# Two decode layers with a cached attention: where two weight blocks and two kept quarters lie, and how one V load is split

## The chip, the cores and the metric

The kernel runs on one core of a Trainium2 chip. The time is the device time of one execution in microseconds (us); of several runs the median is given. In the traces, TensorE is PE (its weight loads PEld), VectorE is DVE, ScalarE is ACT, and SP is the engine that issues the loads.

## The reference

One token goes twice through the same two blocks: attention with 32 heads over a cache of 4096 keys and values, and a small MLP. All is float32.

```python
# x (1,1,512); k_cache, v_cache (1,32,4096,128); wq (512,4096); wo (4096,512)
def A(x, k, v, wq, wo):
    q = (x @ wq) per head                       # (1,32,1,128)
    p = softmax(q . k * 128**-0.5)
    return (p . v) over all heads @ wo
def B(x, w1, b1, w2, b2):
    return gelu(x @ w1 + b1) @ w2 + b2
x = x + A(layernorm(x), ...)
x = x + B(layernorm(x), ...)
x = x + A(layernorm(x), ...)
x = x + B(layernorm(x), ...)
```

The cache is 134 MB. Both layers read it, and what fits into the core's memory between the two isn't read again.

## The kernel before

**Tiles.** The heads are worked on in 8 groups of 4. K or V of one group is a block of 128 partitions by 16384 elements (8.39 MB). It is cut into 8 chunks, and a chunk into 4 quarters, one for each head of the group. `U` is the width of a quarter (512), `NC = 4 * U` that of a chunk. So a place such as `C_AT + 22 * U` lies in the middle of chunk 5 of block C. wq and wo of one group take a chunk's room each; two such that lie side by side in memory are loaded as one `pair` (2.10 MB).

**Places.** One large tile, `arena`, holds three blocks A, B and C, and behind them `SHARED`, a scratch place and `PAIR`, where the pair lies at most times.

**A group.** `scores` multiplies the queries with K, chunk by chunk (4 matmuls for a chunk). `exponentials` and `weights` make the softmax on VectorE and ScalarE and turn it with 4 transposes on TensorE. `values` multiplies with V, again 8 chunks of 4 matmuls. `head_out` projects with wo (4 matmuls), and `next_queries` makes the next group's queries with wq (4 matmuls). TensorE does this in program order.

**Order of the loads.** `load` issues a DMA on SP's queue, in program order. SP waits with each load until the place it writes is free, that is until the last reader of all that it covers has ended; the loads behind it wait along with it. Loads of the K and V blocks go round A, C and B.

**The second layer** goes through the groups backwards, 7 to 0. K of group 7 is still in C and V of group 7 in A, from the first layer. Of V of group 6, 26 quarters were kept in B and the last 6 in PSUM (`pK`). While the scores of group 7 run over C, K of group 6 is loaded into `SHARED`, behind the pair, and into the chunks of C that become free, up to 22U. The pair of wo and wq for group 6 and 5 comes behind it. Then ScalarE copies the 6 kept quarters out of PSUM, two of them into C and four to `PAIR`, and with them group 6 has all that it needs.

With `n = 2`, group 5 begins: its K goes into A, which is free as soon as the values of group 7 have been taken. Its V goes into C, over K of group 6, the pair and the two kept quarters. It is loaded in two parts, and each part waits for its own readers:

```python
for c, t in blocks(v, g, v_home, LAST if final else ((0, 5), (5, 8)) if n == 2 else ((0, C),)):
```

All other blocks up to the last group are loaded whole.

Of the kernel before, what the change touches and what calls it, by code (L numbers as in the profile page):

```python
# [23 lines left out]
C = 8  # L24
# [4 lines left out]
U = 512  # L29
# [7 lines left out]
A_AT, B_AT, C_AT = RING  # L37
# [3 lines left out]
PAIR = SHARED + 11 * U  # L41
# [3 lines left out]
LAST = ((0, 4), (4, 6), (6, 7), (7, 8))  # L45
# [5 lines left out]
def decode_layers(ctx: ExitStack, tc: tile.TileContext, x, k, v, w, w1, b1, w2, b2, out):  # L51
# [13 lines left out]
    def at(first, n):  # L65
        return arena[:, first : first + n]

    def load(first, src):
        t = at(first, src.shape[-1])
        tc.keep_in_program_order(nc.sync.dma_start(t, src))  # L70
        return t
# [4 lines left out]
    def quarters(first):  # L76
        return [at(first + U * j, U) for j in range(4)]

    def part(src, g, a, b):
        return src[g][:, NC * a : NC * b]  # L80

    def of_w(row, i, n):
        return w[row][:, NC * i : NC * (i + n)]

    def by_four(t):
        return t.rearrange("p (j n) -> p j n", j=4)
# [67 lines left out]
    def idle(to, n=U):  # L154
        matmul(to[:, :n], zero[:, 0:1].to_broadcast([P, P]), at(C_AT, n), start=True, stop=True)
# [34 lines left out]
    def scores(z, c, kt):  # L190
        for j in range(J):
            matmul(pS[32 * j : 32 * j + C, :], z[:, j, C - 1 - c : 2 * C - 1 - c], kt[j],
                   start=(c == 0), stop=(c == C - 1))

    def exponentials(sc, nsc):
        nc.vector.tensor_reduce(ml[:, 0:1], pS, axis=AX.X, op=ALU.max)  # L196
        mt, m, bias = small("mt", 32), small("m"), small("mt", 32)
        nc.vector.transpose(mt, ml)
        nc.vector.tensor_reduce(m, mt[:, :C], axis=AX.X, op=ALU.max)
        nc.vector.tensor_scalar(mb[:, :C], m.to_broadcast([P, C]), nsc, None, op0=ALU.mult)  # L200
        nc.vector.transpose(bias, mb)  # L201
        p = at(SCRATCH, U)
        nc.scalar.activation(p, pS, AF.Exp, bias=bias[:, 0:1], scale=sc, accum_out=ml[:, 0:1])  # L203
        return p

    def weights(p):
        for b in range(4):
            tc.keep_in_program_order(nc.tensor.transpose(  # L208
                pT[:, b].rearrange("p j r -> p (j r)"), p[:, P * b : P * (b + 1)], ident))
        pt = work.tile([P, P], F32, name="turned").rearrange("p (j c b) -> p j c b", j=J, c=C)  # L210
        nc.vector.tensor_copy(pt, pT[:, :, :, :C].rearrange("p b j c -> p j c b"))  # L211
        lt, l, lr, rl = small("mt", 32), small("l"), small("mt", 32), small("rl")
        nc.vector.transpose(lt, ml)  # L213
        nc.vector.tensor_reduce(l, lt[:, :C], axis=AX.X, op=ALU.add)
        nc.vector.tensor_copy(lb, l.to_broadcast([P, 32]))
        nc.vector.transpose(lr, lb)
        nc.vector.reciprocal(rl, lr[:, 0:1])
        return pt, rl

    def values(i, pt, vt, c):  # L220
        for j in range(J):
            matmul(pO[32 * j : 32 * j + 4, :], pt[:, j, c, :], vt[j],
                   start=(i == 0), stop=(i == C - 1))

    def head_out(rl, wt, last=False):
        ot = at(SCRATCH, U)
        nc.vector.transpose(ot, pO)  # L227
        o, on = small("o", 4), on_wide
        own = at(SCRATCH, 4 * 129).rearrange("p (b q) -> p b q", q=129)[:, :, :P]
        own = own.rearrange("p b (d q) -> p d b q", q=32)[:, :, :, 0]  # L230
        nc.vector.tensor_reduce(o, own, axis=AX.X, op=ALU.add)  # L231
        if last:
            nc.vector.tensor_scalar(on[:, :4], o, rl, None, op0=ALU.mult)
        else:
            nc.vector.tensor_scalar(in_quarters(on, 4), o.unsqueeze(1).to_broadcast([P, J, 4]), rl, None,  # L235
                                    op0=ALU.mult)
        for d in range(4):
            if last:
                for j in range(J):
                    matmul(pS[32 * j : 32 * j + 1, :P], on[:, d : d + 1], wt[:, d, P * j : P * (j + 1)],  # L240
                           start=(d == 0), stop=(d == 3))
            else:
                matmul(pO, on[:, d : d + P], wt[:, d, :], start=(d == 0), stop=(d == 3))
        return of_32(turned(pS) if last else turned(pO, wide=True), 4)
# [34 lines left out]
    def load_w1(first, a, b):  # L279
        load(first + W1C * a, w1[:, W1C * a : W1C * b])  # L280

    def load_w2(first, a, b):
        load(first + U * a, w2[:, U * a : U * b])
# [4 lines left out]
    def blocks(src, g, home, pieces=((0, C),)):  # L288
        for a, b in pieces:
            load(home + NC * a, part(src, g, a, b))  # L290
            for c in range(a, b):
                yield c, quarters(home + NC * c)
# [15 lines left out]
    def next_queries(n, xs, negm, wt):  # L308
        for c in range(4):
            matmul(pO, xs[:, 2 * c : 2 * c + P], wt[:, c, :], start=(c == 0), stop=(c == 3))  # L310
        return queries(n, negm, wide=True)

    def add_up(acc, own):
        t = small("acc", 4)
        nc.vector.scalar_tensor_tensor(t, own, 1.0, acc, op0=ALU.mult, op1=ALU.add)
        return t
# [4 lines left out]
    for g in range(G):  # L321
        final = g == G - 1
        k_home, v_home = RING[2 * g % 3], RING[(2 * g + 1) % 3]
# [3 lines left out]
        for c, t in blocks(v, g, v_home, LAST if final else ((0, C),)):  # L327
# [3 lines left out]
            if g == G - 2:  # L331
                for j in range(J):
                    i = 4 * c + j - KEPT_V // U
# [8 lines left out]
        else:  # L342
            pair = load(PAIR, of_w(g % 2, g, 2))
# [11 lines left out]
    g = G - 2  # L355
# [5 lines left out]
    def begin_k(home, n):  # L361
        a = len(k_t)
        load(home, k[g][:, U * a : U * (a + n)])
        k_t.extend(at(home + U * i, U) for i in range(n))
# [4 lines left out]
    for c in range(C):  # L369
# [2 lines left out]
            begin_k(C_AT + NC * c, 4)  # L372
        if c == 5:
            begin_k(C_AT + 2 * NC, 14)
    pair = load(C_AT + 22 * U, of_w(g % 2, g - 1, 2))
    p = exponentials(sc, nsc)
    z = next_queries(1, xs, negm, wq_t)
    pt, rl = weights(p)
# [2 lines left out]
    acc = add_up(acc, head_out(rl, wo_t))  # L381

    v_t = [at(B_AT + U * i, U) for i in range(KEPT_V // U)]
    for i, first in enumerate([C_AT + 30 * U, C_AT + 31 * U] + [PAIR + U * j for j in range(4)]):
        t = at(first, U)
        nc.scalar.copy(t, pK[i])
        v_t.append(t)
# [9 lines left out]
    for n in range(2, G):  # L397
        g, final = G - 1 - n, n == G - 1
        k_home, v_home = homes[(2 * n - 1) % 3], homes[2 * n % 3]
        for c, t in blocks(k, g, k_home, HALVES if final else ((0, C),)):  # L400
            scores(z, c, t)
        pt, rl = weights(exponentials(sc, nsc))
        for c, t in blocks(v, g, v_home, LAST if final else ((0, 5), (5, 8)) if n == 2 else ((0, C),)):
            values(c, pt, t, c)
            if final and c > 4:
                idle(pS)
        if final:
            wo_t = by_four(load(PAIR, of_w(g % 2, g, 1)))
            for a, b in W1_AT_END:
                load_w1(A_AT, a, b)  # L410
            for a, b in W2_AT_END:
                load_w2(A_AT + 11 * U, a, b)
            own = head_out(rl, wo_t, last=True)
        else:
            pair = load(PAIR, of_w(g % 2, g - 1, 2))
            acc = add_up(acc, head_out(rl, by_four(pair[:, NC:])))
            z = next_queries(n + 1, xs, negm, by_four(pair[:, :NC]))
# [47 lines left out]
```

## Time and profile before

| | |
|---|---|
| median of 3 runs | 680.22 us (679.94 to 680.78) |
| the profiled execution | 679.55 us, its span 677.8 us |
| TensorE busy | 433.1 us, 64% |
| VectorE busy | 110.7 us, 16% |
| ScalarE busy | 22.2 us, 3% |
| read from HBM | 286.14 MB |
| mean rate over the span | 422 GB/s |

The span runs from the first to the last instruction of the trace. The shares of the engines are means over it. The rate is what the 16 DMA engines of the core read.

### The profile page before, as it was taken

The numbers are of one execution on the slowest core, as the hardware profiler recorded it, in microseconds if no ns is written. First come the engines' busy times: TensorE is split into PE (matmuls) and PEld (weight loads), VectorE is DVE, ScalarE is ACT, GpSimd is POOL, SyncE is SP. The second block draws the span as 40 slices with busy tenths as digits, with TensorE's granted clock in tenths as the row PEclk, the third lists the DMA queues.
The fourth block names the chain that finished last, engine by engine and source line by source line (L and its number), as shares of the span: only waits on it lengthen the run. The fifth ranks groups of instructions, "written<-read, shape, count | busy, mean of one in ns | idle before, by whom it ended". The sixth has DMA issues, their size and how long they took to land. (4 is left out here: it accounts for less than half of the span.)

```text
span 677.8 us, 6359 instructions
## 1 busy us (share of the span) xinstructions
PE 433.1 (64%) x2792; PEld 119.4 (18%) x2792; DVE 110.7 (16%) x431; ACT 22.2 (3%) x47; POOL 4.3 (1%) x21
## 2 busy tenths in 40 slices
PE   1547666485554874667777897686455764766776
PEld 0112112121111211111113222221111111211112
DVE  1012101111021101210212312211021011210211
ACT  0010000000000000001000110000000000000000
POOL 1000000000000000000000000000000000000000
PEclk9969768797698876977979998998698776977977
DMA  9999999999999999999999999899999999999997
GB/s 372 434 433 433 435 433 433 416 449 437 430 433 413 451 433 430 433 431 422 428 413 359 426 459 414 358 468 441 427 433 398 465 433 423 437 430 410 426 416 294
DMA packets 11404, 286.56 MB, mean 423 GB/s; under 512 B 1776, under 2 KB 1776, under 8 KB 3440
## 3 DMA queue, kind: packets, MB, share of 16 engines
q1 hardware_dynamic: 10944, 286.14, 98.7%
q8 instruction: 22, 0.36, 0.2%
q10 hardware_dynamic: 432, 0.01, 0.0%
q14 instruction: 6, 0.05, 0.0%
HBM read 286.14 MB, written 0.00 MB: 422 GB/s over the span
## 5 line engine op out<-in xcount | busy, mean ns | idle before, releaser
L74 PE MATMUL pO<-arena,turned 128*4 128x512 f32 x1024 | 144.8, 726 | 76.8 <-DMA arena<-in_v 75.6
L74 PE MATMUL pS<-arena,zq 128*8 128x512 f32 x1024 | 137.7, 698 | 70.8 <-DMA arena<-in_k 65.4
L74 PE MATMUL pO<-arena,x_wide 128*128 128x512 f32 (+1 forms) x176 | 54.9, 508 | 24.4 <-DVE turned L137 18.1
L74 PE MATMUL pO<-arena,on_wide 128*128 128x512 f32 x112 | 51.8, 605 | 18.6 <-DVE on_wide L235 18.6
L74 PEld LDWEIGHTS pS<-arena,zq 128*8 128x8 f32 x1024 | 29.1, 99 | 176.3 <-issue 167.1
L74 PEld LDWEIGHTS pO<-arena,turned 128*4 128x4 f32 x1024 | 27.6, 97 | 183.8 <-issue 179.5
L137 DVE STREAM_TRANSPOSE turned<-pO 32x128 f32<-32x128 f32 x112 | 35.0, 312 | 101.1 <-PE pO L74 99.9
L227 DVE STREAM_TRANSPOSE arena<-pO 128x512 f32<-128x512 f32 x16 | 11.5, 717 | 220.4 <-PE pO L74 220.4
L208 PE MATMUL pO<-ident,arena 128*128 128x128 f32 x64 | 14.5, 368 | 43.9 <-ACT arena L203 42.4
L196 DVE TENSOR_REDUCE ml<-pS 128x1 f32<-128x512 f32 x16 | 11.1, 692 | 185.0 <-PE pS L74 185.0
L74 PEld LDWEIGHTS pO<-arena,x_wide 128*128 128x128 f32 (+1 forms) x176 | 21.6, 155 | 57.1 <-DVE turned L137 26.5
L203 ACT ACTIVATE arena<-pS,mt,sc 128x512 f32<-128x512 f32 x16 | 12.4, 777 | 523.7 <-DVE mt L201 523.7
L74 PEld LDWEIGHTS pO<-arena,on_wide 128*128 128x128 f32 x112 | 20.1, 189 | 51.7 <-DVE on_wide L235 31.6
L208 PEld LDWEIGHTS pO<-ident,arena 128*128 128x128 f32 x64 | 9.3, 181 | 58.6 <-ACT arena L203 51.3
L74 PE MATMUL pO<-arena,x 128*2 128x344 f32 x64 | 7.2, 531 | 5.0 <-DMA arena<-in_w 4.4
L74 PE MATMUL pS<-arena,zero 128*128 128x512 f32 x16 | 9.9, 706 | 0.0
L74 PE MATMUL pS<-arena,gelu_g 128*1 128x128 f32 x176 | 6.7, 290 | 1.5 <-DVE gelu_g L270 1.3
L213 DVE STREAM_TRANSPOSE mt<-ml 128x32 f32<-128x32 f32 x16 | 3.4, 212 | 17.2 <-ACT arena L203 17.2
L74 PEld LDWEIGHTS pS<-arena,gelu_g 128*1 128x1 f32 x176 | 3.9, 88 | 7.4 <-DVE gelu_g L270 3.7
L211 DVE COPY turned<-pO 128x128 f32<-128x128 f32 x16 | 4.4, 277 | 3.1 <-PE pO L208 3.1
L74 PE MATMUL pO<-arena,zero 128*128 128x512 f32 x8 | 4.5, 644 | 0.0
L248 POOL TENSOR_TENSOR xb<-x,b2c 128x4 f32<-128x4 f32 x2 | 0.4, 200 | 636.9 <-DVE x L148 636.9
(71 smaller groups left out, 76.5 us busy)
## 6 DMA issues: line engine op xcount, KB each, us to landing
arena<-in_w SPq DMA_DIRECT2D x13, 2048.0 KB, 28.8
arena<-in_k SPq DMA_DIRECT2D x4, 4096.0 KB, 42.5
arena<-in_v SPq DMA_DIRECT2D x2, 4096.0 KB, 47.6
arena<-in_w SPq DMA_DIRECT2D x6, 1024.0 KB, 20.3
arena<-in_v SPq DMA_DIRECT2D x1, 5120.0 KB, 23.8
arena<-in_w SPq DMA_DIRECT2D x6, 688.0 KB, 30.2
arena<-in_v SPq DMA_DIRECT2D x2, 2048.0 KB, 50.8
arena<-in_v SPq DMA_DIRECT2D x4, 1024.0 KB, 53.3
```

The lines of the kernel that those rows point to most:

```text
L74: tc.keep_in_program_order(nc.tensor.matmul(*a, **kw))
L137: nc.vector.transpose(t[q], src[q, P * j : P * (j + 1)])
L196: nc.vector.tensor_reduce(ml[:, 0:1], pS, axis=AX.X, op=ALU.max)
L203: nc.scalar.activation(p, pS, AF.Exp, bias=bias[:, 0:1], scale=sc, accum_out=ml[:, 0:1])
L208: tc.keep_in_program_order(nc.tensor.transpose(pT[:, b].rearrange("p j r -> p (j r)"), p[:, P * b : P * (b + 1)], ident))
L211: nc.vector.tensor_copy(pt, pT[:, :, :, :C].rearrange("p b j c -> p j c b"))
L213: nc.vector.transpose(lt, ml)
L227: nc.vector.transpose(ot, pO)
L248: nc.gpsimd.tensor_tensor(xb, pairs(xs)[:, :, 0], b2c, op=ALU.add)
```

## The change

The pair of wo and wq for group 6 and 5 moves from 22U to 24U of C: from the half of chunk 5 to chunks 6 and 7. The first two of the kept quarters of V of group 6 move from 30U and 31U (the end of chunk 7) to 22U and 23U (the second half of chunk 5). V of group 5 is loaded as chunks 0 to 5 and 6 to 7, where it was 0 to 4 and 5 to 7. Nothing else changes; what is computed, and from which bytes, is the same.

```diff
-    pair = load(C_AT + 22 * U, of_w(g % 2, g - 1, 2))
+    pair = load(C_AT + 24 * U, of_w(g % 2, g - 1, 2))
...
-    for i, first in enumerate([C_AT + 30 * U, C_AT + 31 * U] + [PAIR + U * j for j in range(4)]):
+    for i, first in enumerate([C_AT + 22 * U, C_AT + 23 * U] + [PAIR + U * j for j in range(4)]):
...
-        for c, t in blocks(v, g, v_home, LAST if final else ((0, 5), (5, 8)) if n == 2 else ((0, C),)):
+        for c, t in blocks(v, g, v_home, LAST if final else ((0, 6), (6, 8)) if n == 2 else ((0, C),)):
```

On SP, the difference of the two programs from the pair for group 6 (first row) to K of group 4 (last row) is this; a name that begins with DMAHW is the landing of an earlier load, the other names are the counts of an engine's finished work:

```order
 L70 DMA arena<-in_w 128x4096 [waits PE_49]
 L70 DMA arena<-in_k 128x16384 [waits DMAHW0_49,PE_49]
-L70 DMA arena<-in_v 128x10240 [waits DMAHW5_49,DMAHW4_49,DMAHW6_49,DMAHW1_49,PE_49]
-L70 DMA arena<-in_v 128x6144 [waits DMAHW2_49,DMAHW7_49,PE_49,Activation_49]
+L70 DMA arena<-in_v 128x12288 [waits DMAHW4_49,DMAHW5_49,DMAHW1_49,DMAHW6_49,PE_49,Activation_49]
+L70 DMA arena<-in_v 128x4096 [waits DMAHW7_49,DMAHW2_49,PE_49]
 L70 DMA arena<-in_w 128x4096 [waits DMAHW3_49,Activation_49]
 L70 DMA arena<-in_k 128x16384
```

The order of the loads stays. The wait for ScalarE, whose copies fill the kept quarters, has moved from the second part of V to the first; the first part now covers their place, and so it waits for the values that read them. The row of the pair is the same.

On TensorE, in the values of group 5, the difference is this:

```order
 L208 MATMUL pO<-ident,arena 128x128 x3
 L74 MATMUL pO<-arena,turned 4x512 [waits DMAHW1_49,DVE_49]
-L74 MATMUL pO<-arena,turned 4x512 x19
+L74 MATMUL pO<-arena,turned 4x512 x23
 L74 MATMUL pO<-arena,turned 4x512 [waits DMAHW2_49]
-L74 MATMUL pO<-arena,turned 4x512 x11
+L74 MATMUL pO<-arena,turned 4x512 x7
 L74 MATMUL pO<-arena,on_wide 128x512 [waits DMAHW3_49,DVE_49]
 L74 MATMUL pO<-arena,on_wide 128x512 x3
```

The matmuls are the same. The wait for the second part of V has moved from the first matmul of chunk 5 to the first of chunk 6.

## Rows read from the trace of the kernel before

**Rows 1.** The page: TensorE's busy time; DMA share in 40 slices, in tenths.

```profile
PE 433.1 (64%) x2792; PEld 119.4 (18%) x2792; DVE 110.7 (16%) x431; ACT 22.2 (3%) x47; POOL 4.3 (1%) x21
DMA  9999999999999999999999999899999999999997
```

**Rows 2.** Windows: length, engines' busy us (instructions); last PE clock, DMA share, GB/s.

```profile
4.00:345.00 341.00, 201.29 (x1164) 54.39 (x1168) 50.39 (x191) 11.41 (x23) 0.99 (x4) 0.82 1.00 431
426.00:436.00 10.00, 8.36 (x63) 2.42 (x65) 1.48 (x5) 0.00 (x0) 0.00 (x0) 1.00 0.82 319
416.00:446.00 30.00, 22.53 (x144) 6.44 (x136) 6.65 (x24) 0.87 (x2) 0.00 (x0) 0.94 0.97 406
445.00:645.00 200.00, 126.03 (x716) 33.67 (x708) 31.90 (x114) 4.16 (x10) 0.00 (x0) 0.83 1.00 432
```

**Rows 3.** TensorE's waits from 445 us on: us in total, times, longest.

```profile
PE pO L74 <- DMA arena<-in_v: 28.7, 5, 7.4
PE pS L74 <- DMA arena<-in_k: 18.9, 5, 5.0
```

**Rows 4.** The chain that ended last, its end: start, us, what.

```profile
655.95 17.85 DMA arena<-in_w
...
675.29 0.17 DVE y L421
```

**Rows 5.** Timeline of SP: start and length of an issue, us.

```profile
394.39 0.33 SPq L70 DMA_DIRECT2D arena<-in_k  x1
...
406.36 0.33 SPq L70 DMA_DIRECT2D arena<-in_v  x1
...
428.80 0.33 SPq L70 DMA_DIRECT2D arena<-in_v  x1
...
429.65 0.43 SPq L70 DMA_DIRECT2D arena<-in_k  x1
```

**Rows 6.** Issue to landing, us: issues at 394.39, 406.36, 428.80; first load; output.

```profile
arena<-in_k SPq DMA_DIRECT2D x1, 23.7
...
arena<-in_v SPq DMA_DIRECT2D x1, 5120.0 KB, 23.8
...
arena<-in_v SPq DMA_DIRECT2D x1, 3072.0 KB, 9.8
...
arena<-in_w SPq DMA_DIRECT2D x1, 1024.0 KB, 5.1
...
out<-y SPq DMA_DIRECT2D x1, 2.0 KB, 1.4
```

**Rows 7.** Timeline of TensorE: values of groups 7, 6; scores, values 5; scores 4.

```profile
387.27 7.05 PE L74 MATMUL pO<-arena,turned 128*4 128x512 f32 x64 [0.39 <-DVE turned L211]
...
410.19 8.40 PE L74 MATMUL pO<-arena,turned 128*4 128x512 f32 x64 [0.38 <-DVE turned L211]
...
430.35 7.05 PE L74 MATMUL pS<-arena,zq 128*8 128x512 f32 x64 [1.64 <-DVE zq L186]
...
441.55 8.09 PE L74 MATMUL pO<-arena,turned 128*4 128x512 f32 x64 [0.38 <-DVE turned L211]
...
464.49 8.56 PE L74 MATMUL pS<-arena,zq 128*8 128x512 f32 x64 [4.74 <-DMA arena<-in_k]
```

**Rows 8.** Timeline of ScalarE: two kept quarters copied, and the exponential behind.

```profile
381.28 1.07 ACT L386 COPY arena<-pK 128x512 f32<-128x512 f32 x2 [16.46 <-PE pS L74]
382.96 0.78 ACT L203 ACTIVATE arena<-pS,mt,sc 128x512 f32<-128x512 f32 x1 [0.60 <-DVE mt L201]
```

**Rows 9.** Timeline of the weight loads: last of group 6's scores and values.

```profile
405.29 0.11 PEld L74 LDWEIGHTS pS<-arena,zq 128*8 128x8 f32 x4 [0.32 <-issue]
...
416.70 0.10 PEld L74 LDWEIGHTS pO<-arena,turned 128*4 128x4 f32 x4 [0.33 <-issue]
417.13 0.10 PEld L74 LDWEIGHTS pO<-arena,turned 128*4 128x4 f32 x4 [0.33 <-issue]
417.56 0.10 PEld L74 LDWEIGHTS pO<-arena,turned 128*4 128x4 f32 x4 [0.33 <-issue]
```

## The prediction

> **What bounds the kernel now.** Read the page first. TensorE is busy 64% of the span, while the DMA line stands at 9 in all slices but two [rows 1]. The reader is to see a kernel that is one long stream of loads. Next come the windows: the stream moves 431 GB/s from 4 to 345 us and 432 from 445 to 645, with a DMA share of 1.00 [rows 2]. From 445 us on TensorE waits five times for a K load and five times for a V load, so every one of the five groups left waits for its loads [rows 3]; and the chain that ended last closes with a 17.85 us wait for the last weights and under 2 us of work behind it [rows 4]. So a microsecond in which the stream stands still in the second layer is a microsecond at the end, and nothing else counts.
>
> The change touches one place where it does stand still. In 426 to 436 us the rate is 319 GB/s; over 416 to 446 it is 406 [rows 2]. Against 432 that is 10 x (1 - 319/432) = 2.6 us and 30 x (1 - 406/432) = 1.8 us of standstill. The issues of the loads say why [rows 5, 6]. K of group 5 (8.39 MB) is issued at 394.39 and lands 23.7 us later, at 418.1. The first part of V of group 5 (5.24 MB) is issued at 406.36 and lands at 430.2: 12.1 us behind K, which is just 5.24 MB at 432 GB/s, so the stream runs on without a hole. The second part (3.15 MB) is issued only at 428.80 and lands at 438.6: 8.4 us behind the first, where its bytes need 7.3. Its place holds wo and wq, and the last projection that reads them ends just before 428.8, as the scores of group 5 begin at 430.35 behind a transpose [rows 7]. By the landings, which the slowest engine sets, the hole is 1.1 us; by bytes over all engines 1.8 to 2.6. From issue to landing the second part took 9.8 us, that is 2.5 us beyond its bytes: this I call the restart.
>
> **The change, part by part.**
>
> The pair of wo and wq moves from 22U to 24U in C. Before and after it overlaps chunk 7 of the scores, so its issue waits for the same matmuls (in the listing its row is the same). Cost 0.
>
> Two kept quarters go to 22U and 23U, in chunk 5. Their copies may start two chunks of scores (7.05 us for eight chunks [rows 7]) or 1.8 us sooner than at 381.28. ScalarE has nothing else until the exponential at 382.96 [rows 8], and values of group 6, which read the copies, begin at 410.19 [rows 7]. Cost and gain 0; were that cover gone, two copies cost 1.07 us.
>
> The split of V of group 5 at six chunks makes the first part 6.29 MB and the second 2.10 MB, the same bytes. The two are still issued one behind the other on SP, and behind them stand the next pair and K of group 4 (429.65) [rows 5]. What changes is which reader frees each. The second part still covers the pair, so it is still free at 428.80. The first part now covers 22U and 23U. These hold the kept quarters 26 and 27, and they are read by chunk 6 of the values of group 6. So the first part no longer goes out behind the scores, at 406.36, but behind chunk 6 of the values.
>
> When is that? The weight loads of these values stand in groups of four, two for a chunk; the last chunk's are at 417.13 and 417.56, chunk 6 ends with the one at 416.70 [rows 9]. From the last group to the issue that it frees takes 1.07 us, as the scores show (405.29 to 406.36) [rows 5, 9]. So the first part is issued at 416.70 + 1.07 = 417.8, 11.4 us later than now.
>
> At that time only 0.3 us of K of group 5 are left (it lands at 418.1), and SP has issued nothing behind it. The old cover, 11.7 us of K still to come at 406.36, is gone, and the stream stops here instead. With the restart of 2.5 us the first part lands at 417.8 + 2.5 + 6.29 MB/432 GB/s = 417.8 + 2.5 + 14.6 = 434.9. A stream without a hole would have landed it at 418.1 + 14.6 = 432.7, so the new hole is 2.2 us. In return the old one closes: at 428.80 the first part has 6 us to go, the second part follows without a gap, 4.9 us for 2.10 MB, and lands at 439.7. Now it lands at 438.6. All that follows is 1.1 us later.
>
> The same sum, shorter: both kernels restart the stream once, at 428.80 or at 417.8. After the later restart 3.15 MB of V remain, after the earlier one 8.39. The difference of 5.24 MB takes 12.1 us, and TensorE needs only 428.80 - 417.77 = 11.0 us between the two releases. 12.1 - 11.0 = **+1.1 us**. The restart cancels if it costs the same at both places.
>
> TensorE itself loses nothing: values of group 5 start at 441.55 and take 8.09 us [rows 7], so they need the first part by 441.55 (lands 434.9) and the second, now at chunk 6 and not 5, by about 447 (lands 439.7).
>
> **Bounds.** The trace has no restart from a queue that is all but empty in this place. The nearest rows: the 2 KB output took 1.4 us from issue to landing, and the first load of the program, 1.05 MB, 5.1 us, that is 2.7 beyond its bytes [rows 6]. With 1.4 the sum is 0.0, with 2.7 it is +1.3. I take 2.5, since it is the same queue, the same kind of transfer and the same engines 11 us away. The moment of release hangs on TensorE's clock: these values took 8.40 us, those of group 7 took 7.05 at 387.27 [rows 7]. Were they 1.35 us quicker in another execution, the first part would go out at 416.4, but the projection behind them would end 1.35 us sooner too, for either kernel: the difference of 1.1 stays, and the time would come to -0.25 against the before seen here.
>
> The rate is the other term. The rows give 431 and 432 GB/s over 341 and 200 us [rows 2]. The Trainium skill, "DMA: Bandwidth & Descriptors", section "Where 436 GB/s comes from", says that for transfers from HBM to SBUF the HBM side, about 358 GB/s, binds, and not the fabric's 435. By that figure K of group 5 would still be under way long after 417.8, neither split would leave a hole, and the sum would be 0. The trace does not agree: 432 is near the page's fabric figure, and the hole is there.
>
> **The numbers.** The profiled execution took 679.55 us, 677.8 of it the span and 1.75 around it; it should become 680.6. It lies 0.67 below the median of the runs, 680.22, so the median should become 680.22 + 1.1 = **681.3 us**. I count as no change what is within 0.2%, 1.36 us; +1.1 is 0.16%.
>
> **Rivals.**
>
> Faster: the hole closes and none opens. Place: the issue of the first part. To follow K of group 5 without a gap it would have to go out by 415.6 (418.1 less the restart). Then the second part lands 1.1 us sooner by the landings, 1.8 to 2.6 by bytes: 677.6 to 679.1, about 678.4. For it: the bigger first part does cover the wait at 428.80. Against it: the release at 417.8 is 2.2 us too late, and even the quicker values give 416.4. Chance 0.07.
>
> Slower by over 0.2%: a restart out of an empty queue costs more than the one seen, where 1.4 us of the first part were still in flight at 428.80. From 2.8 us up the loss passes 1.36 us. With the first load's 2.7 it is 681.5, with 3.2 it is 682.0. For it: the first load is the only one that starts on an empty queue. Against it: 2.7 and 2.5 lie close. Chance 0.21.
>
> No difference: K of group 5 lands late enough to cover the new wait, or the restart is as cheap as the output's 1.4 us. It would need K to land 2.2 us later than its row, at 420.3, or a slower stream; then before would have no hole either. 680.2. Chance 0.05. (The rule of the Trainium skill's DMA page above ends here; the rows on the rate speak against it.)
>
> **How the numbers follow.** The forecast, +1.1 us and within 0.2%, has 0.67. Same: 0.67 + 0.05 = 0.72; slower 0.21; faster 0.07. The range goes from the cheap restart (680.2) less the 0.3 by which the fastest run lies under the median, 679.9, to the dear one (681.5) plus the 0.6 by which the slowest lies above it, 682.1. It holds all but the faster rival and the ends of the slower one, under 2 in 10.
>
> **What the profile after will show.** The first part of V of group 5 (6144 KB) issued near 417.8, released by matmuls into pO, 17 us to landing; the second (2048 KB) near 428.8, about 11 us to landing. The rate falls in 414 to 422 and is full in 426 to 436. Scores of group 4, which now wait for their K until 464.49 [rows 7], start about 1.1 us later, and so does each stage behind; the two copies of ScalarE start near 379.5. An issue of the first part at 416 or sooner, or scores of group 4 no later than now, would make the prediction wrong; so would a shift at the end that is not there at group 4.

## The result, and the profile after

The changed kernel takes 681.73 us in the median, the kernel before 680.43 in the same comparison (22 runs each): a ratio of 1.0018, with a 95% interval from 1.001 to 1.0027. By the ratio that is 1.2 us slower, from 0.7 to 1.8. The forecast was +1.1.

The profiled execution of the changed kernel has a span of 680.1 us. These are its lines on TensorE's share and on the DMA engines in 40 slices, from the page:

```profile
PE 429.3 (63%) x2792; PEld 119.3 (18%) x2792; DVE 110.4 (16%) x431; ACT 22.2 (3%) x47; POOL 4.3 (1%) x21
DMA  9999999999999999999999998999999999999996
```

One slice is at 8 again, but it is another one: the 25th (408 to 425 us) and no longer the 26th (424 to 441) [rows 1]. The windows show the same move (columns as in [rows 2]); the first row is of the kernel before, the four others of the changed one:

```profile
414.00:422.00 8.00, 6.67 (x49) 1.93 (x42) 1.13 (x3) 0.00 (x0) 0.00 (x0) 1.00 0.92 396
414.00:422.00 8.00, 6.67 (x50) 1.91 (x39) 1.13 (x3) 0.00 (x0) 0.00 (x0) 1.00 0.78 299
426.00:436.00 10.00, 8.36 (x62) 2.31 (x64) 1.48 (x5) 0.00 (x0) 0.00 (x0) 1.00 0.96 410
416.00:446.00 30.00, 22.53 (x132) 6.50 (x128) 6.65 (x24) 0.87 (x2) 0.00 (x0) 0.89 0.95 399
445.00:645.00 200.00, 126.33 (x720) 33.91 (x712) 31.39 (x112) 3.48 (x8) 0.00 (x0) 0.83 1.00 431
```

From 426 to 436 us the stream now runs at 410 GB/s, where it ran at 319; from 414 to 422 it stands still for a part of the time (299, where it was 396). From 445 us on it is full as it was. The 30 us around both show 399 GB/s in place of 406, but that difference decides nothing: a kernel below that loads as before does (the places alone) has 392 and 390 there.

The timeline of SP shows the issues of K of group 5 and of the two parts of its V, and below it is the time from issue to landing of each, in the same order:

```profile
394.18 0.33 SPq L70 DMA_DIRECT2D arena<-in_k  x1
...
417.61 0.33 SPq L70 DMA_DIRECT2D arena<-in_v  x1
...
428.49 0.33 SPq L70 DMA_DIRECT2D arena<-in_v  x1
```

```profile
arena<-in_k SPq DMA_DIRECT2D x1, 25.9
...
arena<-in_v SPq DMA_DIRECT2D x1, 6144.0 KB, 18.5
...
arena<-in_v SPq DMA_DIRECT2D x1, 2048.0 KB, 12.5
```

The first part went out 11.3 us later than in [rows 5], the second 0.3 sooner. On TensorE and ScalarE these rows of the timeline belong to it (the end of chunk 6, the values of group 5, the scores of group 4; the two copies):

```profile
416.46 0.10 PEld L74 LDWEIGHTS pO<-arena,turned 128*4 128x4 f32 x4 [0.33 <-issue]
...
441.38 9.55 PE L74 MATMUL pO<-arena,turned 128*4 128x512 f32 x64 [0.38 <-DVE turned L211]
...
465.35 9.52 PE L74 MATMUL pS<-arena,zq 128*8 128x512 f32 x64 [4.29 <-DMA arena<-in_k]
```

```profile
379.35 1.07 ACT L386 COPY arena<-pK 128x512 f32<-128x512 f32 x2 [14.75 <-PE pS L74]
```

The last group of weight loads of chunk 6 is at 416.46; 1.07 us later is 417.53, and the issue came at 417.61. The values of group 5 waited for the softmax and not for a load. The copies started 1.9 us sooner, and nothing followed from that.

The executions differ by a microsecond or two before they come to this place, so one number serves for all kernels below: **the stage**, from the issue of K of group 5 (TensorE sets it, at the end of group 7's values) to the first scores of group 4, which wait for their K. Before it is 464.49 - 394.39 = 70.1 us [rows 5, 7]; in the changed kernel it is 465.35 - 394.18 = 71.2. The difference is +1.1 us.

A second number goes with it. The trace holds 16 marks for the landing of each load, the updates of the load's semaphore, which no view prints one by one. They are read here as one for each of the 16 DMA engines. The time from issue to landing in the views, and with it the stage, goes by the last mark alone. For K of group 4 the marks lie between 462.19 and 464.35 us before and between 463.26 and 465.21 in the changed kernel. **The mean mark** of K of group 4, counted from the issue of K of group 5 as the stage is, tells where the whole stream stands and not its slowest engine: 68.3 us before, 69.8 in the changed kernel, a difference of +1.4.

### The profile page after: what moved, and what is told of

It reads as the page before. It is cut to its first block, busy times and chain, and to the rows that moved or that the text cites. A ratio compares the mean times of both kernels' runs of the same rounds, so it can differ in the third digit from the quotient of the medians.

```text
span 680.1 us, 6360 instructions
## 1 busy us (share of the span) xinstructions
PE 429.3 (63%) x2792; PEld 119.3 (18%) x2792; DVE 110.4 (16%) x431; ACT 22.2 (3%) x47; POOL 4.3 (1%) x21
## 5 line engine op out<-in xcount | busy, mean ns | idle before, releaser
L74 PE MATMUL pO<-arena,turned 128*4 128x512 f32 x1024 | 143.1, 719 | 80.7 <-DMA arena<-in_v 79.5
## 6 DMA issues: line engine op xcount, KB each, us to landing
arena<-in_v SPq DMA_DIRECT2D x1, 6144.0 KB, 18.5
```

The lines of the kernel that those rows point to most:

```text
L74: tc.keep_in_program_order(nc.tensor.matmul(*a, **kw))
```

## The experiments

The theory on trial: the second layer is a stream of loads, and what counts is when it restarts after it has run dry, and how many bytes are left then. The rivals: the new places cost by themselves (theory 2), or the sizes of the two parts do (theory 3). All kernels were timed against the kernel before, with the stage and the mean mark read from one profiled execution of each.

| kernel | first part out, us | second (third) | stage, us | mean mark, us | against before: ratio (interval) | us |
|---|---|---|---|---|---|---|
| before | 406.4 | 428.8 | 70.1 | 68.3 | 1 | |
| changed | 417.6 | 428.5 | 71.2 | 69.8 | 1.0018 (1.001 to 1.0027) | +1.2 |
| changed, again | 417.9 | 428.8 | 71.4 | 69.7 | 1.0018 (1.0004 to 1.0032) | +1.2 |
| places alone | 407.8 | 430.6 | 69.9 | 68.7 | 0.9987 (0.9974 to 1.0001) | -0.9 |
| places alone, again | 407.5 | 430.2 | 70.0 | 68.6 | 1.0 (0.9986 to 1.0013) | 0.0 |
| split alone | 427.1 | 428.8 | 80.1 | 78.6 | 1.0134 (1.012 to 1.0148) | +9.1 |
| chunk 6 last | 419.0 | 429.0 | 72.1 | 70.6 | 1.0031 (1.0018 to 1.0044) | +2.1 |
| chunk 6 first | 412.8 | 429.6 | 69.5 | 67.0 | 0.998 (0.9967 to 0.9992) | -1.4 |
| three parts | 407.8 | 419.9 (430.4) | 67.6 | 66.7 | 0.9986 (0.9972 to 0.9999) | -1.0 |
| three parts, again | 406.5 | 418.4 (428.9) | 68.3 | 66.8 | 0.9983 (0.9971 to 0.9995) | -1.2 |
| cut at 22U | 406.9 | 429.6 | 71.1 | 67.7 | 0.9997 (0.9987 to 1.0007) | -0.2 |
| cut at 22U, again | 406.4 | 430.3 | 70.3 | 68.6 | 0.9989 (0.9976 to 1.0002) | -0.7 |

The last column is the ratio by the 681 us of before. The stage and the mean mark don't always agree, since the last mark of K of group 4 came 0.8 to 3.3 us behind the mean one. Where they differ the mean mark is the better guide: from it to the mean mark of the last weights it took 210.7 us in all twelve executions, within 0.04 us, so what the stream has lost or gained by K of group 4 stands unchanged at its last load.

**One half of the change at a time.** The places alone, with the old split:

```diff
-        ... LAST if final else ((0, 6), (6, 8)) if n == 2 else ((0, C),)):
+        ... LAST if final else ((0, 5), (5, 8)) if n == 2 else ((0, C),)):
```

> The pair and the two kept quarters lie as in the changed kernel, but V of group 5 is split at chunk 5 as before. Theory 1, the loss is the time in which the load stream stands still because the first part waits for chunk 6 of the values: the first part is free behind the scores again (issue near 406.4), the second near 428.8, the hole is the old one, and the time is that of before, 0.0 us. Theory 2, the new places cost by themselves (copies, waits on ScalarE, other addresses): slower than before by 1.2 us, as the whole change was.

The stage came to 69.9 us, that of before. The whole was 0.9 us faster, with an interval that just took in 1; so it was run again:

> The new places with the old split a second time: 0.9 us faster than before the first time, with an interval that just takes in no change. If the places do nothing: 69.9 us from the issue of K of group 5 to the scores of group 4 as the first time, and an interval around 0.0 us. If they gain by themselves (copies that may start sooner): again 0.9 us faster.

Stage 70.0, ratio 1.0. No cost and no gain of the places is seen. The second interval reaches 0.9 us either way, and the +1.2 of theory 2 lies outside both, so theory 2 falls. The first part was free behind the scores in both; its issue in the first:

```profile
407.81 0.33 SPq L70 DMA_DIRECT2D arena<-in_v  x1
```

The split alone, with the places of before:

```diff
-        ... LAST if final else ((0, 5), (5, 8)) if n == 2 else ((0, C),)):
+        ... LAST if final else ((0, 6), (6, 8)) if n == 2 else ((0, C),)):
```

> The places of before, and only the split at chunk 6. The first part now covers half of wq, so it is freed by the second matmul of the last projection, near 427.9. Theory 1: the stream restarts at 427.9 with 8.39 MB of V to go instead of at 428.8 with 3.15 MB: 12.1 - 0.9 = 11.2 us slower than before. Theory 3, the sizes of the two parts cost by themselves: slower by about 1.2 us only, as the whole change was.

It cost 9.1 us (8.2 to 10.1), the stage 10.0. The windows and the timeline of SP of this kernel show a stream that stands still for 10 us and more:

```profile
416.00:426.00 10.00, 7.28 (x39) 2.32 (x28) 2.54 (x8) 0.00 (x0) 0.00 (x0) 1.00 0.00 0
```

```profile
427.05 2.11 SPq L70 DMA_DIRECT2D arena<-in_v  x2
```

The size is that of theory 1 and not the 1.2 of theory 3, but the expectation was 1.2 too high, and the timeline says why: the first part was out at 427.05, not at 427.9. The part covers the first two chunks of wq, and the second of the projection's four steps of 0.93 us (3.70 us in all) frees it, not the third. Counted from the issue of K of group 5, that is 32.5 us, and the second part of before went out at 34.4. With that, 12.1 - (34.4 - 32.5) = 10.2 us; the stage shows 10.0 and the mean mark 10.3.

**When the first part is freed.** Two kernels are the changed one, with its places and its sizes, but with the values of group 6 in another order of chunks. Chunk 6 first:

```diff
-    for c in range(C):
-        values(c, pt, v_t[4 * c : 4 * c + 4], c)
+    for i, c in enumerate((6, 0, 1, 2, 3, 4, 5, 7)):
+        values(i, pt, v_t[4 * c : 4 * c + 4], c)
```

> The changed kernel, its places and its split at chunk 6, but the values of group 6 take chunk 6 first, then 0 to 5 and 7 (the sum is over the same products in another order). The kept quarters at 22U and 23U are read first, so the first part is freed near 411.9 and not 417.7. Theory 1: K of group 5 covers the restart and no hole is left in either place: faster than before by 1.1 to 2.6 us, and than the changed kernel by 2.3 to 3.8. Theories 2 and 3: as the changed kernel, +1.2 us.

Chunk 6 last, where the order is (0, 1, 2, 3, 4, 5, 7, 6):

> The changed kernel, but the values of group 6 take chunk 6 last (0 to 5, 7, 6), so the kept quarters are read 0.9 us later and the first part is freed near 418.5 in place of 417.6. Theory 1: the stream restarts 0.9 us later with the same 8.39 MB to go. From the issue of K of group 5 to the first scores of group 4 (70.1 us before, 71.2 in the changed kernel) it takes 72.0 us, and the whole is 1.9 to 2.1 us slower than before. Theory 3 (sizes of the parts): as the changed kernel, 71.2 us and +1.2.

The kernel with chunk 6 last was 2.1 us slower than before (1.2 to 3.0), its stage 72.1 us where 72.0 was expected. Its first part went out here:

```profile
418.96 0.33 SPq L70 DMA_DIRECT2D arena<-in_v  x1
```

The one with chunk 6 first was 1.4 us faster than before (0.5 to 2.2), with the same bytes in the same two parts at the same places; so theory 3 falls too. Its stage is shorter by only 0.6, its mean mark by 1.3: the last mark was 2.4 us behind the mean one in this execution, where it was 1.6 before. Here are the issue of its first part and its window:

```profile
412.77 0.33 SPq L70 DMA_DIRECT2D arena<-in_v  x1
```

```profile
416.00:446.00 30.00, 22.52 (x144) 6.29 (x136) 6.57 (x24) 0.87 (x2) 0.00 (x0) 0.94 0.99 418
```

The stream moves 418 GB/s over the 30 us, against 399 and 386 in the changed kernel and 381 with chunk 6 last. From first to last the order of eight chunks is worth 3.5 us.

**Three parts.** Then the new places do have a use: the first part as before, chunk 5 by itself, and chunks 6 and 7.

```diff
-        ... LAST if final else ((0, 6), (6, 8)) if n == 2 else ((0, C),)):
+        ... LAST if final else ((0, 5), (5, 6), (6, 8)) if n == 2 else ((0, C),)):
```

> The new places, and V of group 5 in three parts: chunks 0 to 4, chunk 5, chunks 6 and 7. Theory 1: the first part is issued near 406.4 (behind the scores), the second near 417.7 (behind chunk 6 of the values), while the first is still under way to 430, the third at 428.8 with 3.7 us of the stream still to go. No hole but perhaps a small one, as a restart took 2.5 us: faster than before by 1.1 us (by the landings) to 2.6 (by the bytes). Theories 2 and 3 (places or sizes cost): not faster than before, +1.2 us.

> The kernel in three parts a second time, since its first interval reached from 0.9972 to 0.9999. Theory 1: 67.6 us from the issue of K of group 5 to the scores of group 4, as the first time, within 1 us, and 1.1 to 2.6 us faster than before over the whole. If the gain of the stage is given back later: the same 67.6 us, and no difference over the whole.

The window, the issues of V of group 5 and the scores of group 4 in the first of the two:

```profile
416.00:446.00 30.00, 22.53 (x141) 6.28 (x136) 6.58 (x24) 0.87 (x2) 0.00 (x0) 0.94 1.02 427
```

```profile
407.79 12.47 SPq L70 DMA_DIRECT2D arena<-in_v  x2
...
430.44 0.33 SPq L70 DMA_DIRECT2D arena<-in_v  x1
```

```profile
463.42 7.05 PE L74 MATMUL pS<-arena,zq 128*8 128x512 f32 x64 [1.96 <-DMA arena<-in_k]
```

No hole is left (427 GB/s; 433 in the second). The stage was 2.5 us shorter than before, 1.8 the second time. The whole was 1.0 and 1.2 us faster, at the lower end of what was expected (the first just under it), with both intervals below 1. This kernel and the one with chunk 6 first beat the kernel before, and by the ratios the changed one too. Of the gain of the stage 0.6 to 1.5 us did not reach the end: behind the stage this kernel took 678.0 - 463.42 = 214.6 us in the profile, before took 677.8 - 464.49 = 213.3. The stream gave nothing back. The mean mark had gained only 1.7 and 1.5 us, which lies in both intervals of the whole, and it kept that gain to the last weights. The rest of the stage's 2.5 was the last engine, 0.8 us behind the mean here and 1.6 before.

**Fewer bytes behind the same restart.** The places of before, and V cut where K of group 6 ends, so that the second part has 2.62 MB and not 3.15:

```diff
+    def in_two(src, g, home, n):
+        load(home, src[g][:, :n])
+        load(home + n, src[g][:, n:BLOCK])
+        for c in range(C):
+            yield c, quarters(home + NC * c)
...
-        for c, t in blocks(v, g, v_home, LAST if final else ((0, 5), (5, 8)) if n == 2 else ((0, C),)):
+        vt = blocks(v, g, v_home, LAST if final else ((0, C),))
+        for c, t in in_two(v, g, v_home, 22 * U) if n == 2 else vt:
             values(c, pt, t, c)
```

> The places of before, and V of group 5 cut at 22U, where K of group 6 ends and the pair begins: the first part 5.77 MB (free behind the scores, as before), the second 2.62 MB (free near 428.8, as before). Theory 1: the same restart at the same time with 0.52 MB less to go, so 1.2 us less: 68.9 us from the issue of K of group 5 to the scores of group 4, and 1.2 us faster than before. Theory 3: another size of parts, slower than before or the same.

> The cut at 22U a second time: it was to be 1.2 us faster than before and came to 0.2, with K of group 5 landing 25.6 us after its issue (23.7 before), so that one late DMA engine and not the restart set the landing of the second part. If that is why: where K lands within 24 us, 69 to 69.5 us from the issue of K of group 5 to the scores of group 4, else near 71; over the whole 0.2 to 1.2 us faster than before. If the restart costs the same whatever is left to go: 70.1 us, no difference.

Both times it missed: 1.2 us were expected, 0.2 and 0.7 measured, both intervals with 1 in them. In the first profile K of group 5 landed at 420.5 in place of 418.1, and the first part at 433.8, after the second had been issued at 429.6. In the second K landed after 24.6 us, and TensorE reached the release 35.9 us behind the issue of K, where before it took 34.4. With K that late the expectation called for a stage near 71; it came to 70.3, close to the 70.1 of its rival. The stage can't tell the two apart. The mean mark can: from the issue of the second part to the mean mark of K of group 4 it took 33.0 and 32.7 us here, and 33.9 before and in both executions of the places alone. That is 0.9 and 1.2 us less, near the 1.2 that theory 1 says. Part of it was used up before the restart, as TensorE reached the release 0.3 and 1.5 us later than in the kernel before. So the sum holds for this cut too, but over the whole the cut is not shown to gain.

**The changed kernel again**, beside the last two:

> The changed kernel itself beside the two others, so that all three are compared on one chip. Theory 1: 71.2 us from the issue of K of group 5 to the scores of group 4, and 1.1 to 1.2 us slower than before; 1.1 slower than the new places with the old split.

Its stage was 71.4 us, and it was 1.2 us slower than before and, by the ratios, than the places alone in the same comparison. In this execution K landed at 418.4, near the 418.1 of the one from which the forecast was made. Its issue of the first part, its landing and the window:

```profile
417.87 0.33 SPq L70 DMA_DIRECT2D arena<-in_v  x1
```

```profile
arena<-in_v SPq DMA_DIRECT2D x1, 6144.0 KB, 18.2
```

```profile
414.00:422.00 8.00, 6.67 (x49) 1.93 (x42) 1.13 (x3) 0.00 (x0) 0.00 (x0) 1.00 0.58 209
```

## Why the prediction was right, point by point

**The bound.** What the stream loses is lost at the end. The split alone emptied it for 10 us and the kernel became 9.1 us slower, while the new places, which move copies on ScalarE and addresses, changed nothing that could be seen.

**The release.** Predicted 417.8, measured 417.6 and 417.9. That chunk 6 of the values sets it was shown by moving that chunk: 412.8 and faster when it is first, 419.0 and slower still when it is last. The second part was out at 428.5 and 428.8, as predicted.

**The sum.** 5.24 MB at 432 GB/s less the time between the two releases: 12.1 - 11.0 = 1.1. The stage grew by 1.1 and 1.3 us, the mean mark by 1.4 both times, the whole by 1.2 both times. In all nine executions in which the stream ran dry (before, the places alone, the changed kernel, the split alone, chunk 6 last, the cut at 22U) the mean mark of K of group 4 came 2.3 to 2.6 us later than the release plus the time of the bytes then left, up to the end of that load. So the mechanism of the forecast holds: a release, a restart, and the bytes behind it. That the stage met the forecast to 0.1 us is partly luck: the slowest engine, 0.8 to 3.3 us behind the mean mark, alone moves it by more.

**The restart** is the term that was mis-sized. It was taken as 2.5 us, put the landing of the first part at 434.9, and was said to cancel. The first part landed at 436.1 in both executions of the changed kernel: from issue to landing it took 18.5 - 14.6 = 3.9 us beyond its bytes, and 3.6 in the second (18.2). But that is its last mark. By the mean mark the restart took 2.5 and 2.4 us, against 2.2 in the kernel before, so it did nearly cancel; the 0.2 to 0.3 us by which it did not are why the mean mark grew by 1.4 and not by 1.1.

What the prediction had wrong is to read a landing, which is that of the slowest engine, as the place of the whole stream. The second part of before has its 16 marks within 0.6 us, so there the two nearly agree; the first part of the changed kernel has them over 2.0 and 1.8. For the same reason both holes were read too small. By the mean marks the old one is 2.2 us and not the 1.1 on which its sum went (its other reading, 1.8 to 2.6 by the bytes, was the better one), and the new one 3.6 in the second execution and not 2.2. The error is about the same in both, so it falls out of the difference. It also explains why the second part landed 2.6 and 2.4 us behind that of before, counted from the issue of K of group 5, and K of group 4 only 1.1 and 1.3: by the mean marks the lag is 1.4 at both places, and in the kernel before the marks spread again, from 0.6 us at the second part to 2.2 at K of group 4. Why one engine falls behind the others is not shown.

**Nothing on TensorE.** Right: the values of group 5 took 9.55 us in place of 8.09, at a mean granted clock of 0.73 against 0.87, and it cost nothing, since the scores of group 4 still waited 4.29 us for their K.

**The rivals.** The faster one was wrong for this change but right as a mechanism: closing the old hole without a new one gains 1.0 to 1.4 us over the whole (three parts, chunk 6 first) and 1.3 to 1.7 by the mean mark, so between its 1.1 by the landings and its 2.6 by the bytes. The dearer restart came true for the last engine and by only 0.2 to 0.3 us for the stream, so it did not decide. The rival of no difference had its condition all but met in the first execution of the changed kernel, where K of group 5 landed at 420.0 (it asked for 420.3), and the loss came all the same: 14 of the 16 marks were there by 418.1, and the two late ones did not keep the stream full (299 GB/s from 414 to 422 us). The slow stream is excluded by 431 GB/s over 200 us. The Trainium skill, "DMA: Bandwidth & Descriptors", section "Where 436 GB/s comes from", has HBM's 358 GB/s bind for such loads; the trace does not agree and lies near the fabric's 435 of that section.

## What to carry to other kernels

When loads bound a kernel, a part of a load starts with the last reader of all that it covers: one quarter with a late reader holds back everything that is loaded with it, and everything queued behind. To see what a new split is worth, write down for each the time at which the stream restarts and the bytes then left; the difference of the bytes' time and of the releases is the answer. Held against the mean mark it was right to 0.3 us here; the landing of a single load, which waits for its slowest engine, leaves a microsecond or more of doubt. And before cutting sizes anew, look whether the late reader can read sooner: here one chunk read first instead of seventh was worth 2.6 us.

## What was not expected of the hardware

The landing of one and the same 8.39 MB load, issued at a time that TensorE sets and into a stream that was full, came 23.6 to 25.9 us after its issue in twelve executions; by the mean of its marks, 22.1 to 23.4. A part issued as the stream ran dry took 2.5 to 4.4 us beyond its bytes by its last mark, but 2.2 to 2.5 by the mean one, whether it was 2.62, 3.15 or 6.29 MB and whether the stream had stood still for a moment or for 10 us. So most of what looks like a change in the price of a restart is the lateness of one or two engines. In eight of these nine executions the marks of the part behind the stop lay closer together than those of K of group 5 ahead of it (in the kernel before 0.6 us against 2.1).
